# Two experts of a routed layer in passes of 224 and 160 columns, and the conversion of the last weights dealt out anew

## The chip, the cores and the metric

One core of a Trainium2 chip runs the kernel. The metric is the device time of one execution in microseconds; lower is better.

## What is computed

Attention over 4 x 8 heads with a window of 32 around each of 512 local tokens and 32 global tokens (2176 tokens of 512 features in all), then a routed layer of eight experts, then a dense layer with a rational function between its two products. Cut to the part around the change:

```python
e_idx = np.argmax(x @ w_gate, axis=1)
for e in range(E):                      # E = 8
    mask = e_idx == e
    h = np.maximum(x[mask] @ w1[e], 0.0)          # 512 -> 1024
    out[mask] = gate_w[mask, None] * eom[mask, e, None] * (h @ w2[e])   # 1024 -> 512
...
h = x @ w_in                                       # 512 -> 2048
g = P(h) / (Q(h) + 1e-6)
return g @ w_out                                   # 2048 -> 512
```

The reference's inputs (seed 0) route 422, 331, 253, 249, 220, 149, 434 and 118 tokens to the eight experts.

## The kernel before, in words

Every product is made in three parts from a high and a low half of each float32 operand (`fp32r`), so a matrix of weights is first split: ScalarE copies a piece of 128x512 to the high half (line 695), VectorE or GpSimd subtracts to give the low half (line 699, odd pieces on VectorE, even ones on GpSimd).

**Experts.** `expert(e)` (line 1023; the text counts from the first, so e = 4 and 5 are the fifth and sixth) runs one wide pass (`wide`, line 918) over a fixed number of token columns, `wd(e)`: 256, or what `WIDE` (line 43) names. Tokens beyond that are done after it in a branch (`beyond`, line 1031), which is entered only if the count is larger. A pass has eight blocks of hidden features. For block s: 12 matmuls into a PSUM tile `ph` (line 932; there are two such banks), the ReLU on ScalarE (line 937), the low half on VectorE (line 938, which is the last reader of `ph`), and, two blocks later, 12 matmuls of the second product (line 944). At the end ScalarE and VectorE copy the four sums to the tile `yt` (line 950), and ScalarE's queue stores `yt` to memory (line 869, reached from line 954).

**The plan.** While expert e runs, a plan (`PLANW`, line 61) is woven between its matmuls: 32 places, four for each block from the third on (two after each half of the first product, two in the second product). At its places stand: `s` splits the next weights piece of the next expert, whose load SP's queue issues four pieces ahead (line 685); `g` gathers rows of tokens (line 804); `x` and `p` scale, transpose and split tokens for the next expert (lines 816, 829, 809, 810); `c` does one step of the conversion.

**The conversion.** 18 pieces of the last layer's weights come as 64-bit floats and are turned to 32 bits in three VectorE steps each (`conv_step`, line 748; lines 731, 734, 737). After the third step SP's queue stores the piece (line 755) and loads the next but one (line 757). Piece q is written into `self.f32[q % 3 % 2]`: a tile of its own, `f32`, or, where q mod 3 is 1, the first 512 numbers of each partition of `yt` (`spare`, line 1001). The tile framework makes each write wait for the readers of what it overwrites, stores included. Each of the second to seventh expert does three pieces (nine steps), at places 2 to 4, 12 to 14 and 22 to 24; `todo` (line 962) counts on from step 9(e - 1).

```python
self.conv_op(self.r64[q % 2], self.f32[q % 3 % 2], n)
if n == 2:
    CQ(self.nc).dma_start(out=self.wf[q], in_=self.f32[q % 3 % 2].bitcast(F32))
```

Of the kernel before, what the change touches and what calls it, by code (L numbers as in the profile page):

```python
# [24 lines left out]
E = 8  # L25
# [14 lines left out]
NB = 2  # L40
BASE, MOST, LAG = 256, 512, 2
NX = 4
READY, WIDE = (6,), {0: 296, 1: 332, 6: 308}
FIRST = WIDE[0]
SA, S0, S1 = "v", "a", "a"

# [1 line left out]
def plan(n, **at):  # L48

    o = [""] * n  # L50
    for t in "scxpgk":
        for k in at.get(t, ()):
            o[k] += t
    return o


NPRE, NCONV = 2, 9

LOADS = [(f, f + 1) for f in range(0, NPRE, 2)] + [(f,) for f in range(NPRE, 16)]
WLO = lambda nc, f: nc.vector if f < 3 else nc.gpsimd  # L60
PLANW = plan(32, s=range(0, 31, 2), c=(2, 3, 4, 12, 13, 14, 22, 23, 24), g=(1, 3, 18, 24), x=(1, 2, 14, 16), p=(5, 8, 19, 22))
PLANW7 = plan(30, s=(0, 5, 6, 8, 9, 11, 12, 14, 15, 17, 18, 20, 21, 23, 24, 25))
EY = 11, 1, 11, 1
GT = 25, 27
# [39 lines left out]
class Build:  # L104
# [731 lines left out]
    def experts(self, st, first, gate):  # L836
# [8 lines left out]
        wd = lambda e: WIDE.get(e, BASE)  # L845
# [12 lines left out]
        X = lambda e: self.xs if e == 0 else self.xa if e % 2 else self.x2c  # L858
# [8 lines left out]
        def store(e, c, n, y, q):  # L867

            q.dma_start(out=self.ybuf[:, :, bass.ds(off[e] + c, n)], in_=y)
# [48 lines left out]
        def wide(e, n, x, bg, last=True, acc=None, before=None):  # L918

            W = self.slot[e % 2]  # L920
            nh = min(NH, 1 + (NH - 1) * BASE // n)
            rest, bg = bg, iter(()) if before else bg
            acc = [ps_a.tile([128, 512], F32, tag=f"acc{m}", name=f"acc{m}") for m in range(4)] if acc is None else acc
            for s in range(8 + LAG):
                if s == AFTER and before:
                    before()
                    bg = rest
                if s < 8:
                    ph = ps_h.tile([128, 512], F32, tag="ph", name="ph")[:, :n]
                    c = 128 * (s % 4)  # L930
                    for i, (k, a, b) in enumerate(ORDER):
                        nc.tensor.matmul(ph, lhsT=W[:, b, 2 * k + s // 4, c:c + 128], rhs=x[:, a, k, :n],  # L932
                                         start=(i == 0), stop=(i == 11))
                        if i % 6 == 5:
                            next(bg, None)
                    hi, lo = (hT(s % nh, n)[:, a] for a in range(2))
                    nc.scalar.activation(hi, ph, AF.Relu)  # L937
                    nc.vector.scalar_tensor_tensor(out=lo, in0=ph, scalar=0.0, in1=hi.bitcast(F32),
                                                   op0=ALU.max, op1=ALU.subtract)
                if s >= LAG:  # L940
                    f = s - LAG
                    for m in range(4):
                        for i, (a, b) in enumerate(PAIRS):
                            nc.tensor.matmul(acc[m][:, :n], lhsT=W[:, b, 8 + f, 128 * m:128 * m + 128],  # L944
                                             rhs=hT(f % nh, n)[:, a], start=(f == 0 and i == 0), stop=(f == 7 and i == 2))
                        if m % 2:
                            next(bg, None)
            def end():
                for m in range(4):
                    (nc.scalar.copy, nc.vector.tensor_copy)[m % 2](yt[:, m, :n], acc[m][:, :n])  # L950
                k = min(NBLK, 128 - NBLK * e)
                YQ(nc).dma_start(out=self.toks[bass.ds(off[e], 128 * k), :].rearrange("(j p) o -> j (p o)", p=128),
                                 in_=self.idxT[NBLK * e:NBLK * e + k])
                store(e, 0, n, yt[:, :, :n], YQ(nc))

            if last:
                end()
            for _ in bg:
                pass
            return end  # L960

        def todo(e, plan, half=None, blocks=(), gathers=(), mode=SPLIT_MODE):


            sp = self.split_set(e + 1, mode if e < E - 1 else MODE7, half)
            k = NCONV * (e - 1)
            gs, xs, ps, ns = iter(gathers), iter(blocks), iter(blocks), self.counts()
            for do in plan:
                for c in do:
                    if c == "s":  # L970
                        next(sp, None)
                    elif c == "c":
                        self.conv_step(k)
                        k += 1
                    elif c == "k":
                        next(ns, None)
                    elif c == "g":
                        for e2, b, j in filter(None, islice(gs, 1)):
                            self.gather(j, col(e2, b))
                    elif c == "x":  # L980
                        for e2, b, j in filter(None, islice(xs, 1)):
                            self.scale(j, 128, S0 if e == 0 else S1)
                    elif c == "p":
                        for e2, b, j in filter(None, islice(ps, 1)):
                            if e2:
                                self.prep(j, X(e2), ps_t(), 128 * b, scale=False, pt=None if e else next(turns)())
                            elif b == FIRST // 128:
                                self.prep(j, self.xs, ps_t(), 0, scale=False, skip=FIRST % 128, pt=next(turns)())
                            else:
                                self.prep(j, self.xs, ps_t(), 128 - FIRST % 128, FIRST % 128, scale=False, pt=next(turns)())  # L990
                yield

        blocks = lambda e, bs=range(4): [(e, b, b) for b in bs if e < E]

        def fetch(e, i):

            ixo = self.ixo[:, 0:1]
            nc.gpsimd.tensor_copy(ixo, self.idx[:, bass.ds(i + NBLK * e, 1)])
            self.gather(NX - 1, ixo)
# [14 lines left out]
        def weave(*gens):  # L1014
            gens = list(gens)
            while gens:
                for g in list(gens):
                    try:
                        next(g)
                    except StopIteration:  # L1020
                        gens.remove(g)
                yield

        def expert(e, early=lambda: ()):

            plan = PLANW if e < E - 1 else PLANW7
            more_ = blocks(e + 1, (2, 3)) if e + 1 in READY else [None] * 2
            wide(e, wd(e), X(e), weave(todo(e, plan, None, blocks(e + 1, (0, 1)) + more_, more_ + blocks(e + 2, (0, 1))),
                                         iter(early())), before=(lambda: beyond(e - 1)) if e > 1 else second)

        def beyond(e):
            n, end = wd(e), nc.s_assert_within((cnt[e] + 127) // 128, 0, NBLK)

            def blocks_from(j):
                fetch(e, j)
                more(e, j, end)
            with tc.If(cnt[e] > n):
                if e in READY:
                    single(e, n, X(e), n)
                    with tc.If(cnt[e] > n + 128):  # L1040
                        blocks_from((n + 128) // 128)
                else:
                    blocks_from(n // 128)

        def woven():

            g, sp, end = self.gate(B - 1, woven=GW), todo(0, PLANA, 0, mode="act"), object()
            while True:
                more_ = [next(g, end) for _ in range(GS)]
                next(sp, None)  # L1050
                yield
                if end in more_:
                    break
            ready = [(0, 2, 3)] + blocks(1, (0, 1, 2)) + [(0, 3, 3)]
            yield from weave(sp, todo(0, PLANB, 1, ready, ready + blocks(2, (0, 1)), mode=MODEB),
                             self.lists(), todo(0, PLANC))
# [27 lines left out]
        for e in range(1, E - 2):  # L1084
            expert(e)


        def early():
            for n in range(CH[0]):
                for _ in range(EY[n]):  # L1090
                    yield
                self.load_y(n, nc.scalar)
# [21 lines left out]
        def first_w():  # L1114
            for f in range(NPRE):
                w, (hi, lo) = self.raws[9, 0][:, 512 * f:512 * f + 512], (self.slot[1][:, a, f, :] for a in range(2))
                nc.scalar.copy(hi, w)
                nc.vector.tensor_tensor(out=lo, in0=w, in1=hi.bitcast(F32), op=ALU.subtract)

        expert(E - 2, early)  # L1120
        expert(E - 1, lambda: first_steps([0]))
        beyond(E - 1)
# [3 lines left out]
        with tc.If(rare[0] > 0):  # L1126

            k, w = 128 - NBLK * (E - 1), yt.rearrange("p m t -> p (m t)")[:, 0:NCOL - 128]
# [341 lines left out]
```

## Time and profile before

| what | value |
|---|---|
| median of 3 runs | 778.91 us (778.0 to 779.42) |
| the profiled execution | 779.69 us |
| its span, first to last instruction | 778.0 us |
| mean granted clock of TensorE | 0.993 |
| busy: TensorE, VectorE, ScalarE, GpSimd | 757.1, 584.4, 527.3, 352.7 us |
| the passes of the second to eighth expert start at | 181.54, 226.72, 250.47, 274.72, 298.42, 323.52, 351.98 us |
| the last layer's own stage starts at | 394.76 us |

Times below are microseconds from the start of the span. A matmul's end is modelled, and a row of several matmuls runs from the first one's start to the last one's end; two neighbours overlap. The releaser in brackets is what ended the idle time before an instruction.

### The profile page before, as it was taken

How to read it: one execution, taken by the hardware profiler on the slowest of the kernel's cores; microseconds unless marked ns; L12 is line 12 of the kernel's file. 1: busy time of each engine (PE TensorE's matmuls, PEld its weight loads, DVE VectorE, ACT ScalarE, POOL GpSimd, SP SyncE). 2: the span in 40 equal slices, each digit the busy share in tenths (PEclk: the TensorE clock that was granted, in tenths of full speed). 3: DMA queues.
4: the chain of work that ended last, by engine and by line, in shares of the span. 5: the costliest groups of instructions: out<-in, count | busy, mean ns of one | idle time of the engine just before them, and what ended most of it. 6: DMA issues, size and time to landing. Idle time of an engine off the chain costs nothing. (4 is left out here: it accounts for less than half of the span.)

```text
span 778.0 us, 16683 instructions
## 1 busy us (share of the span) xinstructions
PE 757.1 (97%) x5976; PEld 652.5 (84%) x5976; DVE 584.4 (75%) x1419; ACT 527.3 (68%) x1181; POOL 352.7 (45%) x439
## 2 busy tenths in 40 slices
PE   8998999899999999999999999999999999999996
PEld 5776776698999999998978888898888898989984
DVE  5777788683568877772389998888888768997983
ACT  4666775555455656643778887778777767887872
POOL 4445664523255556541756866532342214322422
PEclk9999999999999999999999999999999999999998
DMA  8998885555588999893463340110010000000101
GB/s 290 323 312 273 291 269 144 144 168 184 191 279 285 316 304 334 287 306 114 127 195 109 109 108 1 51 45 14 1 54 14 1 1 27 28 1 1 40 1 40
DMA packets 51978, 112.55 MB, mean 145 GB/s; under 512 B 10194, under 2 KB 24274, under 8 KB 49832
## 3 DMA queue, kind: packets, MB, share of 16 engines
q1 hardware_dynamic: 42232, 96.39, 39.1%
q0 software_dynamic: 3168, 9.27, 3.4%
q10 hardware_dynamic: 6480, 5.65, 2.3%
q8 instruction: 52, 0.85, 0.5%
q14 instruction: 46, 0.38, 0.2%
HBM read 93.58 MB, written 18.77 MB: 144 GB/s over the span
## 5 line engine op out<-in xcount | busy, mean ns | idle before, releaser
L1256 POOL TENSOR_TENSOR q<-q,ab 128x384 f32<-128x384 f32 (+1 forms) x78 | 93.9, 1204 | 212.1 <-ACT q L1255 205.1
L1295 PE MATMUL acc<-slot,gh 128*128 128x512 f32 x528 | 165.7, 394 | 0.0
L699 POOL TENSOR_TENSOR slot<-raw,slot 128x512 fp32r<-128x512 f32 x66 | 90.3, 1377 | 89.0 <-ACT slot L695 86.9
L1150 PE MATMUL ph<-x2c,slot 128*128 128x512 f32 (+1 forms) x552 | 125.1, 374 | 0.9 <-DVEq L1126 0.6
L1150 PEld LDWEIGHTS ph<-x2c,slot 128*128 128x128 f32 x552 | 101.1, 187 | 19.6 <-DVEq L1126 0.9
L1295 PEld LDWEIGHTS acc<-slot,gh 128*128 128x128 f32 x528 | 98.3, 187 | 20.1 <-ACT gh L1267 0.2
L944 PE MATMUL acc<-hT,slot 128*128 128x256 f32 (+3 forms) x768 | 109.2, 292 | 0.0
L1295 PE MATMUL acc<-slot,gl 128*128 128x512 f32 x264 | 104.4, 395 | 0.0
L944 PEld LDWEIGHTS acc<-hT,slot 128*128 128x128 f32 x768 | 101.9, 189 | 0.2
L695 ACT CAST slot<-raw 128x512 fp32r<-128x512 f32 x128 | 75.0, 618 | 7.6 <-DVE yt L950 4.0
L316 POOL TENSOR_SCALAR pr<-ex,r 128x128 f32<-128x128 f32 x128 | 47.0, 379 | 60.8 <-PE sc L263 21.0
L1150 PE MATMUL ph<-xa,slot 128*128 128x384 f32 x384 | 71.8, 336 | 0.0
L1150 PEld LDWEIGHTS ph<-xa,slot 128*128 128x128 f32 x384 | 67.9, 188 | 2.7
L1267 ACT CAST gh<-u 128x384 fp32r<-128x384 f32 (+1 forms) x78 | 43.3, 555 | 39.0 <-PE acc L1295 20.8
L699 DVE TENSOR_TENSOR slot<-raw,slot 128x512 fp32r<-128x512 f32 x62 | 55.0, 890 | 14.9 <-ACT slot L695 14.4
L1270 ACT ACTIVATE r<-q,cab 128x384 f32<-128x384 f32 (+1 forms) x78 | 51.3, 657 | 19.3 <-POOL q L1256 18.7
L937 ACT ACTIVATE hT<-ph 128x256 fp32r<-128x256 f32 (+3 forms) x64 | 25.7, 401 | 50.8 <-PE ph L932 40.1
L1295 PEld LDWEIGHTS acc<-slot,gl 128*128 128x128 f32 x264 | 49.4, 187 | 12.3 <-DVE gl L1268 0.3
L298 ACT ACTIVATE ex<-sm,mx 128x128 f32<-128x128 f32 x128 | 50.3, 395 | 13.9 <-POOL pr L316 7.0
L1255 ACT ACTIVATE q<-ab,cab 128x384 f32<-128x384 f32 (+1 forms) x78 | 58.3, 747 | 0.9
L1255 ACT ACTIVATE u<-ph,cab 128x384 f32<-128x384 f32 (+1 forms) x78 | 55.0, 705 | 4.0 <-POOL gl L1268 2.8
L932 PE MATMUL ph<-xa,slot 128*128 128x256 f32 (+1 forms) x384 | 54.6, 292 | 1.2 <-PEq L1040 0.4
(235 smaller groups left out, 1471.0 us busy)
## 6 DMA issues: line engine op xcount, KB each, us to landing
raw<-in_w_dram SPq DMA_DIRECT2D x78, 512.0 KB
vw<-in_vw_dram SPq DMA_DIRECT2D x16, 1024.0 KB
r<-in_w_dram SPq DMA_DIRECT2D x18, 512.0 KB
kw<-in_kw_dram SPq DMA_DIRECT2D x16, 384.0 KB
raw<-wf SPq DMA_DIRECT2D x9, 512.0 KB
qt<-in_qT_dram SPq DMA_DIRECT2D x32, 128.0 KB
xbuf<-xrow SPq DMA_DIRECT2D x8, 512.0 KB
xg<-ybuf SPq DMA_DIRECT2D x13, 256.0 KB
```

The costliest lines, as they stand in the source:

```text
L298: nc.scalar.activation(ex[:, h], src[:, h], AF.Exp, bias=mx[:, h:h + 1], scale=-1.0, accum_out=ssum[:, h:h + 1])
L316: nc.gpsimd.tensor_scalar(out=pr[:, h], in0=ex[:, h], scalar1=r[:, h:h + 1], scalar2=1.0, op0=ALU.mult, op1=ALU.mult)
L695: nc.scalar.copy(hi, r)
L699: eng.tensor_tensor(out=lo[:, c], in0=r[:, c], in1=hi[:, c].bitcast(F32), op=ALU.subtract)
L932: nc.tensor.matmul(ph, lhsT=W[:, b, 2 * k + s // 4, c:c + 128], rhs=x[:, a, k, :n], start=(i == 0), stop=(i == 11))
L944: nc.tensor.matmul(acc[m][:, :n], lhsT=W[:, b, 8 + f, 128 * m:128 * m + 128], rhs=hT(f % nh, n)[:, a], start=(f == 0 and i == 0), stop=(f ...
L1150: self.nc.tensor.matmul(ph[:, :w], lhsT=l[a], rhs=r[b], start=(k == 0 and i == 0), stop=(k == 3 and i == 2))
L1255: nc.scalar.activation(o_, x_, AF.Identity, scale=k1, bias=k0)
L1256: nc.gpsimd.tensor_tensor(out=q, in0=q, in1=ab, op=ALU.mult)
L1267: nc.scalar.copy(g[0], up)
L1270: nc.scalar.activation(r0, q, AF.Ln, bias=eps1)
L1295: nc.tensor.matmul(accs[i], lhsT=l[a], rhs=Wo[:, b, f, :], start=(f == 0 and j == 0), stop=(f == 15 and j == 2))
```

## The change

The fifth and sixth expert's passes are 224 and 160 columns wide instead of 256. The conversion is dealt out 4, 3, 3, 2, 2, 4 to the second to seventh expert instead of three to each, at the places that `EACH` gives for the number of pieces. `pair` names the token blocks that an expert has; for every width here it gives the same two as before.

```diff
-READY, WIDE = (6,), {0: 296, 1: 332, 6: 308}
+READY, WIDE = (6,), {0: 296, 1: 332, 4: 224, 5: 160, 6: 308}
...
-NPRE, NCONV = 2, 9
+NPRE = 2
+PIECES = 0, 4, 3, 3, 2, 2, 4, 0
...
-PLANW = plan(32, s=range(0, 31, 2), c=(2, 3, 4, 12, 13, 14, 22, 23, 24), g=(1, 3, 18, 24), x=(1, 2, 14, 16), p=(5, 8, 19, 22))
+EACH = {4: (2, 8, 14, 20), 3: (2, 12, 22), 2: (3, 10), 0: ()}
+PLANW = lambda e: plan(32, s=range(0, 31, 2), c=[k + n for k in EACH[PIECES[e]] for n in range(3)], g=(1, 3, 18, 24), x=(1, 2, 14, 16), p=(5, 8, 19, 22))
...
-            k = NCONV * (e - 1)
+            k = 3 * sum(PIECES[:e])
...
+        pair = lambda e: blocks(e, range(min(2, -(-wd(e) // 128)))) + [None] * (wd(e) <= 128)
...
-            plan = PLANW if e < E - 1 else PLANW7
+            plan = PLANW(e) if e < E - 1 else PLANW7
             more_ = blocks(e + 1, (2, 3)) if e + 1 in READY else [None] * 2
-            wide(e, wd(e), X(e), weave(todo(e, plan, None, blocks(e + 1, (0, 1)) + more_, more_ + blocks(e + 2, (0, 1))),
+            wide(e, wd(e), X(e), weave(todo(e, plan, None, pair(e + 1) + more_, more_ + pair(e + 2)),
```

## Rows read from the trace of the kernel before

**Rows 1.** Stretches of four experts: length; PE, PEld, DVE, ACT, POOL; PEclk, DMA, GB/s

```profile
250.35:274.60 24.25, 24.10 (x203) 23.93 (x201) 19.03 (x30) 14.28 (x31) 13.90 (x11) 1.00 0.92 312
274.60:298.30 23.70, 23.55 (x203) 23.38 (x202) 19.12 (x30) 14.27 (x31) 13.81 (x11) 1.00 0.91 308
298.30:323.40 25.10, 24.95 (x211) 24.78 (x209) 20.20 (x32) 16.63 (x35) 16.78 (x12) 1.00 0.96 331
323.40:351.84 28.44, 28.29 (x203) 28.06 (x201) 20.17 (x30) 15.12 (x31) 12.66 (x10) 1.00 0.90 280
```

**Rows 2.** What PE waited for from 195 to 400 us, the longest of five

```profile
PE ph L1150 <- DVEq L1126: 0.6, 1, 0.6
```

**Rows 3.** Timeline: groups of 12 matmuls; last, durations of single ones of L932

```profile
212.12 1.99 PE L932 MATMUL ph<-xa,slot 128*128 128x332 f32 x12
...
285.70 1.59 PE L944 MATMUL acc<-hT,slot 128*128 128x256 f32 x12
287.12 1.54 PE L932 MATMUL ph<-x2c,slot 128*128 128x256 f32 x12
...
308.28 1.60 PE L932 MATMUL ph<-xa,slot 128*128 128x256 f32 x12
...
L932 PE MATMUL ph<-xa,slot x384: 276/283/419, 181.5 to 390.0; 128*128 128x256 f32 x144, 128*128 128x332 f32 x48
```

**Rows 4.** Timeline of weight loads where PE's stream starts anew, and of transposes (L829)

```profile
367.24 0.19 PEld L932 LDWEIGHTS ph<-xa,slot 128*128 128x128 f32 x1 [0.67 <-issue]
...
367.24 0.30 PEld L932 LDWEIGHTS ph<-xa,slot 128*128 128x128 f32 x2 [0.67 <-issue]
...
176.06 0.20 PEld L829 LDWEIGHTS ph<-ident,xg 128*128 128x128 f32 x2 [0.58 <-issue]
...
180.94 0.14 PEld L829 LDWEIGHTS pt<-ident,xg 40*128 40x128 f32 x1 [0.32 <-ACT xg L816]
...
180.94 0.32 PEld L829 LDWEIGHTS pt<-ident,xg 40*128 40x128 f32 x4 [0.32 <-ACT xg L816]
```

**Rows 5.** DMA queue q10 (ScalarE's): 261.9 to 262.0; 284.7 to 284.9; 227.9 to 234.5

```profile
q10 hardware_dynamic: 2, 0.00, 3.4%
...
q10 hardware_dynamic: 1, 0.00, 0.3%
...
q10 hardware_dynamic: 546, 0.69, 31.4%
```

**Rows 6.** Timeline of the fourth expert's first half: start, us, engine, line

```profile
251.23 0.39 ACTq L869 DMA_DIRECT2D ybuf<-yt  x1
...
255.49 0.42 DVE L731 TENSOR_SCALAR f<-r 128x512 int32<-128x512 int32 x1
...
255.95 0.69 DVE L734 SCALAR_TENSOR_TENSOR f<-r,f 128x512 int32<-128x512 int32 x1
...
257.60 0.42 DVE L938 SCALAR_TENSOR_TENSOR hT<-ph,hT 128x256 fp32r<-128x256 f32 x1 [0.95 <-ACT hT L937]
...
260.35 1.60 PE L932 MATMUL ph<-xa,slot 128*128 128x256 f32 x12
...
262.79 0.42 DVE L731 TENSOR_SCALAR yt<-r 128x512 int32<-128x512 int32 x1
```

**Rows 7.** Timeline of the fifth and the third expert: the store, hidden block 4

```profile
275.49 0.39 ACTq L869 DMA_DIRECT2D ybuf<-yt  x1
...
284.34 1.52 PE L932 MATMUL ph<-x2c,slot 128*128 128x256 f32 x12
...
227.56 0.40 ACTq L869 DMA_DIRECT2D ybuf<-yt  x1
...
236.37 1.54 PE L932 MATMUL ph<-x2c,slot 128*128 128x256 f32 x12
```

**Rows 8.** Two stretches of the attention stage, columns as in rows 1

```profile
67.45:70.86 3.41, 1.54 (x58) 1.15 (x54) 2.07 (x13) 0.80 (x5) 1.46 (x4) 1.00 0.73 260
70.86:74.27 3.41, 3.41 (x35) 2.33 (x35) 1.55 (x8) 1.73 (x8) 1.15 (x3) 0.50 0.45 56
```

## Prediction

> **What bounds the kernel now.** I read the table of stretches first, one row for each expert. The engine columns show TensorE busy for all of every stretch but 0.15 us, VectorE for about four fifths, the DMA engines for 0.90 to 0.96 [rows 1]. Next came what TensorE waited for between 195 and 400 us: five rows, none above 0.6 us [rows 2]. So the experts are paced by the matmul stream, and VectorE and the DMA engines have little to spare. Anything that makes the stream shorter is gained one for one; anything that makes TensorE wait for VectorE is paid one for one.
>
> The stream's pace comes from the groups of 12 matmuls. One matmul reads 0.28 us by itself, 12 read 1.54 to 1.60, so consecutive ones start (1.54 - 0.28)/11 = 115 ns apart in the first product of the fifth expert, 119 in its second, 120 in the sixth; 332 columns give (1.99 - 0.32)/11 = 152 [rows 3], where 0.32 is an estimate from 0.28 and the 76 added columns.
>
> **Narrower passes.** A matmul has its own weight load in this kernel, so the pace has a second limit that a narrow pass does not touch. The trace of before has no such matmul under 256 columns. It does show the load's length: where the stream starts anew, one load reads 0.19 us and two read 0.30, so the second began 0.11 us after the first [rows 4]. A transpose's load is lighter, two in 0.20 [rows 4], that is 0.14 and 0.06. And one place shows what happens when the load outlasts the stream: the 40-column transposes stream for about 20 ns (40/256 of 119), yet their four loads take 0.32 us, (0.32 - 0.14)/3 = 0.06 apart [rows 4]. That is the load's own 0.06, not the stream's 0.02 and not the sum of both. By this the pace falls to the load's 108 to 110 ns and stops there; with a few ns of handover I take 112, whether 224 columns follow or 160.
>
> Each of the two experts has 96 first-product and 96 second-product matmuls. Fifth: 96 x (115 - 112) + 96 x (119 - 112) = 1.0 us. Sixth: 192 x (120 - 112) = 1.5 us. Gain 2.5 us. Lower bound nothing (the pace stays at 119); upper bound in proportion to the columns, 104 and 75 ns: 192 x 13 + 192 x 45 = 11.1 us. But in the sixth the DMA engines bind before that: 331 GB/s for 25.1 us are 8.3 MB [rows 1]; less one converted piece (0.52 MB read, 0.26 MB written) 7.5 MB, 22.7 us at the same rate, so that expert can hardly give more than 2.4 us, and the upper end with DMA is 2.5 + 2.4 = 4.9 us. I take 2.5 because the nearest row with a load longer than its stream follows the load.
>
> The Trainium skill, page "TensorE: Matmul & The Clock Gate", section "Back-to-back issue gap", gives N/2.4 + 2.5 ns for warm matmuls. By that the gaps would be 96 and 69 ns and the gain, as an estimate from that page, 4.0 + 9.8 = 13.8 us; the rows at 256 columns stand at 115 to 120 where it says 109, so the trace does not bear it out here.
>
> The smaller ReLU, subtraction and copies on ScalarE and VectorE gain nothing: TensorE does not wait for them [rows 2]. The smaller stores of those two experts are off the path.
>
> **Pieces dealt anew.** One piece is three VectorE instructions, 0.42, 0.69 and about as much again, a 256 KB store and a 512 KB load on SP's queue. The fifth and sixth lose one each, some 1.8 us of VectorE and 0.79 MB, hidden by TensorE before, so worth nothing by themselves. The second and seventh gain one. The second's stretch is not among the rows; the seventh has 28.44 - 20.17 = 8.3 us of VectorE idle and 280 GB/s where the sixth reached 331 [rows 1]: hidden. Its second piece rewrites the same buffer four plan places after the first; if the store of it is late, VectorE waits, at most by what it has idle: 0, up to 0.5 us for TensorE.
>
> What counts is which buffer each piece uses. Piece q goes to the spare part of yt where q mod 3 is 1. Before, that was the middle piece of each expert, places 12 to 14. With 4 pieces ahead of the third expert the order shifts: pieces 4, 7 and 10 become the FIRST of the third, fourth and fifth expert, at places 2, 2 and 3. But yt is what the expert before has just stored from, and the write must wait for that store. VectorE takes its instructions in order; behind the waiting one stand the subtraction of hidden block 2 (line 938), then the input splits and weight splits. TensorE's hidden block 4 needs the PSUM bank that line 938 frees (two banks).
>
> Fourth expert: the store is issued at 251.23, its last packets move at 261.9 to 262.0 [rows 5], and the old middle piece wrote yt at 262.79 [rows 6]. So the store is done between 262.0 and 262.8; I take 262.4. The new first piece would be due at 255.49 [rows 6]: 6.9 us of wait. Then 0.42 + 0.69, line 938 with 0.42 and 0.1 of gaps: the bank is free at 264.0, where TensorE took it at 260.35 [rows 6]: 3.7 us of stall. The next bank comes after some 2.6 us more of VectorE (five operations like these) against 24 x 0.12 = 2.9 us of TensorE: 0.3 us more at crowded moments. Together 4.0.
>
> Fifth: stored from 275.49, last packets at 284.8 [rows 5, 7], done by 285.2 if as late as in the fourth. At place 3 only one operation stands ahead of line 938: 285.2 + 0.42 + 0.42 + 0.1 = 286.1 against 284.34 [rows 7], less 0.3 that the narrower pass has gained by then: 2.1. Then four more operations of 0.69 and one of 0.42, 3.3 us with gaps, against 24 x 0.112 = 2.7: 0.6. Together 2.7.
>
> Third: stored from 227.56, all 546 packets through by 234.5 [rows 5, 7], done at 234.8; line 938 ends at 236.4 against 236.37 [rows 7]. So 0 at first, 0.4 with crowding after it.
>
> Sum of the stalls 7.1 us. Lower bound: if every store took as little from issue as the third's 7.2 us (227.56 to 234.8), the fourth would be done at 258.4 and the fifth at 282.7, both early enough that TensorE sees nothing: 0. Upper bound: TensorE idle for 3.7 us in one go may lower its clock. After a stretch with 1.54 us of matmuls in 3.41 the granted clock stood at 0.50, the 1.2 GHz level, for 3.41 us [rows 8]; that costs 1.7 us, twice 3.4.
>
> In the sixth, piece 13 writes yt at place 10, about when the store lands there too; what VectorE waits there TensorE does not see, since it needs that bank only a whole block later.
>
> **Sum.** 779.69 (the profiled execution, of which 778.0 are the span) - 2.5 + 7.1 = 784.3; the median of the runs is 0.8 below the profiled one, so 783.5.
>
> **Rivals.**
> The store lands sooner, or VectorE catches up before TensorE looks (the other side). Place: the first piece of the fourth expert. For it: one of the three stores took 7.2 us. Against it: the two that matter took 11.2 and 9.7 under the load that stays there. It decides at 258.7: a store done by then (260.35 less 1.6) costs nothing. Then only the narrow passes are left, with 0.2 of stall: 778.9 - 2.3 = 776.6. Chance 0.17.
>
> The passes go by their columns. For it: 332 to 256 columns is nearly proportional [rows 3]. Against it: the load's 0.11 and the 40-column transposes. With the stalls: 778.9 - 4.9 + 7.1 = 781.1 if DMA binds, 774.9 if it does not. Chance 0.10, of which 0.04 ends below the old time. This is where the rule of the Trainium skill's page would lead.
>
> The stall lowers the clock, or late weight loads follow it (the buffers that VectorE frees late are SP's next loads): 783.5 + 1.7 to 3.4, so 785.2 to 786.9. For it: the row at 0.50 [rows 8]. Against it: the stretch before it held attention's short matmuls, not these. Chance 0.20.
>
> Extra blocks because 224 and 160 are too few: the reference's inputs route 220 and 149 tokens there, so left out.
>
> **Numbers.** Forecast 0.48; the rest 0.05 on either side. A change under 0.2% (1.6 us) is about what a measurement of this kernel cannot tell from none. Faster: most of the first rival's 0.17, 0.04 and a little of the rest, 0.22. Same: 0.10, the part of the forecast and of the second rival between 777.4 and 780.5. Slower 0.68. The range 776.5 to 787.5 takes in the first rival's point, the forecast with stalls of 3 to 9 us, and one clock drop with late loads. The forecast's own range is 780.5 to 786.
>
> **What would show it.** Right: in the third, fourth and fifth expert the first write of yt from the conversion stands right after the store's last packet, with VectorE idle 3, 7 and 5.5 us ahead of it; TensorE then waits for line 938 about 4 us in the fourth and 2 to 3 in the fifth; 12 matmuls of 160 columns read about 1.45 us, as do those of 224. Wrong: no wait of TensorE over 1 us between 226 and 300, or 12 matmuls of 160 columns in 1.1 us or less, or the sixth expert still at 25 us.

## The result, and the profile after

| | median | lowest to highest |
|---|---|---|
| before, 6 runs | 778.45 us | 776.36 to 779.88 |
| after, 6 runs | 803.89 us | 788.76 to 813.81 |

The change makes the kernel slower. The six executions fall in two groups, 788.76 and 789.55 us with a mean granted clock of 0.99 and four from 803.01 to 813.81 us with 0.96 to 0.97; the ratio of the first two to before is 1.0141 [1.0105, 1.0178] (in brackets the 95% interval, here and below), that of the medians 1.033. The profiled execution (806.0 us, span 804.3) is one of the four. Its lower clock belongs to the result: the experiments show that the change brings it about. Lines of the kernel are two further down in the profile after: the first product is line 934, the low half 940, the second product 946.

Where the time went is read from the starts of the passes:

| start of | before | after | later by |
|---|---|---|---|
| third expert | 226.72 | 224.02 | -2.70 |
| fourth | 250.47 | 254.24 | 3.77 |
| fifth | 274.72 | 279.32 | 4.60 |
| sixth | 298.42 | 305.63 | 7.21 |
| seventh | 323.52 | 349.01 | 25.49 |
| eighth | 351.98 | 378.31 | 26.33 |
| last layer | 394.76 | 421.11 | 26.35 |

The 2.7 us ahead of the third expert are not a gain of the change: 2.62 of them lie ahead of the second expert (178.92 against 181.54), in stages that it doesn't touch, and the second, which now converts four pieces, took 45.10 us against 45.18. The third expert lost 6.5, the fourth 0.8, the fifth 2.6, the sixth 18.3, the seventh 0.8.

The table of stretches of the kernel after, third to sixth expert, answers to [rows 1] (length, busy time of PE, PEld, DVE, ACT and POOL with counts, PEclk, DMA share, GB/s). The last two rows are the two stretches at a granted clock of 0.50:

```profile
224.02:254.24 30.22, 25.13 (x203) 24.55 (x201) 20.00 (x29) 14.62 (x31) 13.48 (x10) 0.96 0.75 256
254.24:279.32 25.08, 24.80 (x201) 24.43 (x201) 19.82 (x27) 14.38 (x30) 12.97 (x10) 0.98 0.86 278
279.32:305.63 26.31, 23.46 (x203) 22.68 (x201) 18.65 (x29) 13.08 (x28) 12.25 (x10) 1.00 0.82 264
305.63:349.01 43.38, 42.03 (x211) 41.75 (x209) 16.76 (x28) 17.07 (x37) 17.20 (x13) 0.55 0.59 192
...
251.83:255.24 3.41, 3.30 (x15) 3.30 (x16) 2.11 (x5) 0.74 (x2) 0.00 (x0) 0.50 0.60 184
309.86:350.82 40.96, 40.83 (x191) 40.83 (x192) 15.88 (x28) 15.55 (x33) 15.92 (x12) 0.50 0.53 165
```

The third expert before, which [rows 1] leaves out:

```profile
226.60:250.35 23.75, 23.60 (x202) 23.43 (x202) 19.37 (x29) 14.42 (x31) 12.57 (x11) 1.00 0.87 292
```

The rows tell two stories. In the third and fifth expert TensorE is idle for 5.1 and 2.9 us, and the DMA share is 0.75 and 0.82 where it was 0.87 and 0.91: something waits. In the sixth TensorE is idle for 1.4 us only, but its clock is 0.55: everything it does takes longer.

**The waits.** What TensorE waited for between 195 and 400 us, where before nothing was above 0.6 us [rows 2]:

```profile
PE acc L946 <- DVE hT L940: 3.1, 1, 3.1
PE ph L934 <- DVE hT L940: 3.0, 2, 1.9
PE ph L934 <- DVEq L1041: 2.6, 2, 1.4
```

They are found in the timeline, with what stands ahead of them (VectorE's rows, then two of GpSimd and one of ScalarE, then TensorE's; in brackets the idle time before the instruction and what ended it):

```profile
233.36 1.22 DVE L733 TENSOR_SCALAR yt<-r 128x512 int32<-128x512 int32 x1 [4.25 <-DMA ybuf<-yt]
248.91 1.92 DVE L733 TENSOR_SCALAR f<-r 128x512 int32<-128x512 int32 x1 [2.69 <-DMA wf<-f]
261.10 1.06 DVE L733 TENSOR_SCALAR yt<-r 128x512 int32<-128x512 int32 x1 [1.30 <-DMA raw<-in_w_dram]
277.89 2.52 DVE L739 SCALAR_TENSOR_TENSOR f<-r,f 128x512 int32<-128x512 int32 x1
289.92 1.33 DVE L733 TENSOR_SCALAR yt<-r 128x512 int32<-128x512 int32 x1 [3.89 <-DMA raw<-in_w_dram]
...
249.26 1.27 POOL L701 TENSOR_TENSOR slot<-raw,slot 128x512 fp32r<-128x512 f32 x1
289.69 1.27 POOL L701 TENSOR_TENSOR slot<-raw,slot 128x512 fp32r<-128x512 f32 x1 [1.65 <-ACT slot L697]
...
282.25 0.62 ACT L697 CAST slot<-raw 128x512 fp32r<-128x512 f32 x1 [2.71 <-DVE yt L952]
...
235.69 1.65 PE L934 MATMUL ph<-x2c,slot 128*128 128x256 f32 x12 [1.86 <-DVE hT L940]
251.94 2.50 PE L946 MATMUL acc<-hT,slot 128*128 128x256 f32 x10 [3.08 <-DVE hT L940]
283.95 1.60 PE L934 MATMUL ph<-x2c,slot 128*128 128x224 f32 x12 [1.40 <-DVEq L1041]
291.60 1.60 PE L934 MATMUL ph<-x2c,slot 128*128 128x224 f32 x12 [1.17 <-DVE hT L940]
```

The writes at 233.36, 261.10 and 289.92 are the forecast ones: the first piece of the third, fourth and fifth expert goes to yt and waits for the store from it. (For the last two the view names a weights load as the releaser; the semaphore of the store from yt is set at 261.08 and 289.89, the same moments.) The write at 248.91 was not forecast: pieces 5 and 6 both go to `f`, and piece 6 waits until piece 5 has been stored. Behind it TensorE waits longest, 3.08 us. The wait of 1.40 us at 283.95 has no such write ahead of it: the third step of piece 9, at the end of the fourth expert, took 2.52 us, the copies to yt came after it, ScalarE waited 2.71 us for them, and its ReLU was late.

Part of these stalls is slower work and not waiting. The first step of a piece takes 0.42 us [rows 6], but 1.92 us at 248.91 and 1.33 at 289.92: GpSimd was at work when they began, and each ended 0.3 us after GpSimd's subtraction. Between 180 and 350 us of all the profiles here, the 178 first steps that began while GpSimd was idle took 0.41 to 0.43 us. By that, some 1.5 of the 3.08 us (an estimate, 1.92 less 0.42) are the slower step. No experiment moved GpSimd's work.

The waiting piece also holds up SP's queue. SP's rows of the fifth expert in the kernel after:

```profile
286.12 0.33 SPq L687 DMA_DIRECT2D raw<-in_w_dram  x1
292.90 0.33 SPq L757 DMA_DIRECT2D wf<-yt  x1
293.28 1.27 SPq L759 DMA_DIRECT2D r<-in_w_dram  x1
294.65 1.81 SPq L687 DMA_DIRECT2D raw<-in_w_dram  x2
```

and in the kernel before, in the same expert:

```profile
284.19 5.64 SPq L685 DMA_DIRECT2D raw<-in_w_dram  x3
290.05 0.33 SPq L755 DMA_DIRECT2D wf<-yt  x1
```

After, the store of the piece is next in the queue, its data come late, and SP issues nothing for 6.4 us; the weight loads stand behind it. Before, three loads went out in that time. The queue is not all that held them: there are four weight buffers, and the one that the load at 294.65 fills was still to be read by VectorE's subtraction at 293.39 to 294.07, which itself stands behind the write to yt.

**The clock.** The sixth expert's beginning after (first what stands ahead of the late weight load, then ScalarE, VectorE, TensorE), and a later group of 12 matmuls:

```profile
298.77 0.68 DVE L701 TENSOR_TENSOR slot<-raw,slot 128x512 fp32r<-128x512 f32 x1
298.88 0.33 SPq L757 DMA_DIRECT2D wf<-f  x1
299.78 10.32 SPq L687 DMA_DIRECT2D raw<-in_w_dram  x5
...
306.78 0.62 ACT L697 CAST slot<-raw 128x512 fp32r<-128x512 f32 x1 [3.58 <-DMA raw<-in_w_dram]
308.88 0.30 ACT L939 ACTIVATE hT<-ph 128x160 fp32r<-128x160 f32 x1
309.62 0.32 DVE L940 SCALAR_TENSOR_TENSOR hT<-ph,hT 128x160 fp32r<-128x160 f32 x1
...
309.99 2.85 PE L934 MATMUL ph<-xa,slot 128*128 128x160 f32 x12 [1.20 <-DVEq L1041]
332.10 2.76 PE L934 MATMUL ph<-xa,slot 128*128 128x160 f32 x12
```

ScalarE waits 3.58 us for a weights piece, the ReLU behind it in ScalarE's order is late, and TensorE stands for 1.2 us. The load of that piece went out at 299.78 and landed at 306.70: VectorE's subtraction at 298.77 was the last to read its buffer, and the store of the converted piece went out ahead of it at 298.88. Where TensorE starts again, from 309.86, the granted clock is 0.50, the 1.2 GHz level. Consecutive matmuls then start 213 ns apart (median) for the whole pass, and the clock is back to full only at 350.82, 1.8 us after the seventh expert's 308-column pass has begun.

### The profile page after: what moved, and what is told of

Read it like the earlier page. It is cut to its first block, busy times and chain, and to the rows that moved or that the text cites. A ratio compares the mean times of both kernels' runs of the same rounds, so it can differ in the third digit from the quotient of the medians.

```text
span 804.3 us, 16690 instructions
## 1 busy us (share of the span) xinstructions
PE 775.1 (96%) x5976; PEld 670.3 (83%) x5976; DVE 585.0 (73%) x1419; ACT 526.5 (65%) x1181; POOL 349.8 (43%) x439
## 5 line engine op out<-in xcount | busy, mean ns | idle before, releaser
L701 POOL TENSOR_TENSOR slot<-raw,slot 128x512 fp32r<-128x512 f32 x66 | 88.2, 1345 | 120.5 <-ACT slot L697 116.2
L946 PE MATMUL acc<-hT,slot 128*128 128x256 f32 (+5 forms) x768 | 119.3, 310 | 3.2 <-DVE hT L940 3.1
L946 PEld LDWEIGHTS acc<-hT,slot 128*128 128x128 f32 x768 | 111.8, 209 | 3.8 <-DVE hT L940 3.6
L1154 PEld LDWEIGHTS ph<-xa,slot 128*128 128x128 f32 x384 | 67.9, 188 | 2.7
L939 ACT ACTIVATE hT<-ph 128x256 fp32r<-128x256 f32 (+5 forms) x64 | 24.8, 388 | 62.6 <-PE ph L934 45.9
L934 PE MATMUL ph<-xa,slot 128*128 128x256 f32 (+2 forms) x384 | 62.0, 318 | 2.3 <-DVEq L1041 1.2
L1274 ACT ACTIVATE r<-q,cab 128x384 f32<-128x384 f32 (+1 forms) x78 | 51.2, 657 | 19.1 <-POOL q L1260 18.3
L934 PEld LDWEIGHTS ph<-xa,slot 128*128 128x128 f32 x384 | 58.4, 219 | 3.5 <-DVEq L1041 1.4
```

What stands on the lines that cost most here:

```text
L701: eng.tensor_tensor(out=lo[:, c], in0=r[:, c], in1=hi[:, c].bitcast(F32), op=ALU.subtract)
L1154: self.nc.tensor.matmul(ph[:, :w], lhsT=l[a], rhs=r[b], start=(k == 0 and i == 0), stop=(k == 3 and i == 2))
L1274: nc.scalar.activation(r0, q, AF.Ln, bias=eps1)
```

## Experiments

They undo or isolate the two parts, widths and dealing, then each kind of wait, and then put a pause of TensorE where the clock fell. The kernel before that stands beside each run was timed on the same chip.

### The narrow passes with the old dealing

```diff
-READY, WIDE = (6,), {0: 296, 1: 332, 6: 308}
+READY, WIDE = (6,), {0: 296, 1: 332, 4: 224, 5: 160, 6: 308}
```

> The new widths (224, 160) with the conversion dealt out as before. Waiting theory (the added time is VectorE waiting to write yt): no such wait is left, so 2.5 us faster than before, the sixth expert at about 23.6 us. Clock theory (the 160-column pass, paced by its weight loads, lets the granted clock fall to 0.50): the sixth expert takes about 43 us where that happens, as after the change, so 16 us slower in such an execution; the matmuls stand 213 ns apart there.

Measured: 776.82 us (774.91 to 778.49, 10 runs) against 777.74; ratio 0.9991 [0.9975, 1.0006]. A group of 12 matmuls of 160 columns:

```profile
307.47 1.50 PE L932 MATMUL ph<-xa,slot 128*128 128x160 f32 x12
```

Consecutive ones start 112 ns apart at 160 columns and 111 at 224 (medians). The sixth expert took 24.77 us. In all ten executions the mean granted clock is 0.992 or more: without the new dealing it stayed up here (in a run below with the same widths and dealing, the short pause, one execution of ten lost it). The time is not the 2.5 us less that were expected: the interval reaches from 1.9 us less to 0.5 us more.

### 224 columns in the fifth expert alone

```diff
+READY, WIDE = (6,), {0: 296, 1: 332, 4: 224, 6: 308}
```

> The fifth expert alone at 224 columns, everything else as before. Weight-load theory: its matmuls go from 115 and 119 ns to 112 apart, 1.0 us faster in all. Columns theory: 104 ns, 2.5 us faster. Clock theory: no fall at 224 columns, so the same as the weight-load theory.

Measured: 777.62 us (776.76 to 779.59, 10 runs), ratio 1.0005 [0.9986, 1.0023]. The fifth expert's stretch is 22.70 us long against 23.70 [rows 1]: the forecast 1.0. Over the whole kernel that is less than the measurement can tell.

### The new dealing with the old widths

The kernel after, with `WIDE` as before.

> The conversion dealt out anew, all widths as before. Waiting theory: 7 to 11 us slower than before, in the third to fifth expert, with VectorE idle before the first write of yt. Clock theory: the sixth expert stays near 25 us with the granted clock at 1.00. If the dealing costs nothing, same as before.

Measured: 784.82 us (784.19 to 787.56, 4 runs), ratio 1.0093 [1.0069, 1.0117]. The dealing alone makes about 7 us of the loss. In its profile TensorE waits for the reuse of `f`: 0.68 us behind piece 6 and 3.07 us (at 278.67, in the fourth expert) behind piece 9, which reuses `f` after piece 8. There the clock stood at 0.50 for 6.83 us, with 256 columns, and came back. The write to yt in the fourth kept VectorE 3.09 us, and TensorE did not wait for it.

### The new dealing with each expert's second piece in yt

```diff
+CB = 0, 1, 0, 0, 0, 1, 0, 0, 1, 0, 0, 1, 0, 1, 0, 0, 1, 0
...
-        self.conv_op(self.r64[q % 2], self.f32[q % 3 % 2], n)
+        self.conv_op(self.r64[q % 2], self.f32[CB[q]], n)
```

(and the same in the store). The widths are 224 and 160. In the seventh expert it is the third of the four pieces.

> The changed kernel, but each expert's second piece is the one that goes to yt, as before the change (third to sixth expert: own tile, yt, own tile). Waiting theory: the waits of the third to fifth expert are gone, 7 to 11 us less than the changed kernel; without a fall of the clock 2.5 us faster than before. Clock theory: the sixth expert still takes about 43 us in the executions in which the clock falls. DMA theory (the moved traffic is what costs): no gain against the changed kernel.

Measured: 775.52 us median (773.71 to 793.46, 10 runs); ratio 0.999 [0.9961, 1.002] without the longest. The third and fourth expert in the table of stretches:

```profile
223.80:247.50 23.70, 23.55 (x202) 23.38 (x201) 19.25 (x29) 14.37 (x31) 12.23 (x10) 1.00 0.87 298
247.50:271.80 24.30, 24.15 (x203) 23.98 (x202) 19.30 (x30) 14.28 (x31) 14.28 (x10) 1.00 0.91 312
```

Their lengths, TensorE's time and the DMA share are those of before [rows 1]. So the number of pieces for each expert costs nothing that can be told; the buffer of each piece does. The sixth expert took 23.63 us. One execution of the ten took 793.46 us with a mean granted clock of 0.972; no execution with 224 or 256 columns went so low, so a pass of 160 columns seems to lose the clock now and then even here. That execution has no profile. Another took 783.52 us at 0.993, which stays unexplained.

### The new dealing with 224 and 256 columns

```diff
-READY, WIDE = (6,), {0: 296, 1: 332, 4: 224, 5: 160, 6: 308}
+READY, WIDE = (6,), {0: 296, 1: 332, 4: 224, 6: 308}
```

> The new dealing, fifth expert at 224 columns, sixth back at 256. Theory (stalls by the reused buffers cost about 7 us; the fall of the clock to 0.50 that lasts 41 us needs the 160-column pass of the sixth expert): 783 to 785 us, about 1 below the 784.8 of the new dealing with 256 and 256, no stretch at 0.50 between 220 and 350 us longer than 7 us, in any run. Rival (the stalls alone make the clock stay low, the width has no part in it): some runs above 795 us with a mean granted clock of 0.97, as with 160 columns.

Measured: 785.14 us (784.11 to 787.01, 4 runs), ratio 1.0083 [1.0051, 1.0115], so not the 1 us under the new dealing alone that was expected. In the profile the clock fell once among the experts, for 3.41 us, behind a wait of 3.09 us in the third. The stalls are there, the long fall is not: the mean clock is 0.990 to 0.994 in all four. Only the width of the sixth expert differs from the kernel after. But TensorE's wait at the sixth's beginning is shorter here too, 0.41 us; the version with the scratch tile, below, has the longer one.

### A pause of TensorE before 160, 256 and 224 columns

The old dealing; the low half of the sixth expert's first block is written 12 times, so that TensorE waits for VectorE.

```diff
-                    nc.vector.scalar_tensor_tensor(out=lo, in0=ph, scalar=0.0, in1=hi.bitcast(F32),
-                                                   op0=ALU.max, op1=ALU.subtract)
+                    for _ in range(12 if (e, s) == (5, 0) else 1):
+                        nc.vector.scalar_tensor_tensor(out=lo, in0=ph, scalar=0.0, in1=hi.bitcast(F32),
+                                                       op0=ALU.max, op1=ALU.subtract)
```

> The old dealing with 224 and 160 columns, and the low half of the sixth expert's first tile written 12 times in place of once, so that TensorE waits some 2.5 us for VectorE early in that expert's pass. Theory (a pause lets the granted clock fall, and a 160-column pass does not bring it back): 0.50 for the rest of the pass, some 20 to 35 us of matmuls 213 ns apart, and 776.8 + 2.5 + 12 to 20 = 791 to 799 us. Rival (a pause costs its length and one stretch of 3.41 us at most): 779 to 782 us.

> The same pause, with the sixth expert at 256 columns. Theory: the clock falls for one or two stretches of 3.41 us and comes back within the pass, so 777.6 + 2.5 to 3 + 1.7 to 3.4 = 781 to 784 us. Rival (any pause at this place keeps the clock low, whatever the width): above 790 us, as with 160 columns.

> The pause of before (the sixth expert's first low half written 12 times), with the sixth expert at 224 columns, which run at the same pace of 111 to 112 ns as 160 at the full clock. Theory (it is how few columns stand behind one weight load that keeps the clock down, and 224 are enough): the clock comes back within the pass, 780 to 785 us, as with 256 columns (782.4). Rival (any pass that is bound by its weight loads stays at 0.50 after a pause): 795 us or more, as with 160 columns (798.7).

| columns of the sixth expert | median | lowest to highest | runs | ratio to before |
|---|---|---|---|---|
| 160 | 798.67 | 796.0 to 804.19 | 4 | 1.0244 [1.0209, 1.0279] |
| 224 | 784.46 | 784.17 to 787.23 | 4 | 1.0082 [1.0061, 1.0104] |
| 256 | 782.43 | 779.73 to 786.25 | 10 | 1.0052 [1.0033, 1.0071] |

The pause was about twice as long as meant, and of similar length in the three. TensorE's wait with 160 columns, and the stretches from its fall on:

```profile
PE ph L932 <- DVEq L1038: 5.4, 1, 5.4
...
302.99:346.03 43.04, 39.02 (x184) 39.02 (x185) 20.83 (x40) 14.68 (x32) 15.53 (x12) 0.50 0.61 200
350.78:376.51 25.73, 25.73 (x185) 25.73 (x185) 18.51 (x26) 13.13 (x27) 11.19 (x8) 1.00 0.72 232
```

With 256 columns:

```profile
PE ph L932 <- DVEq L1038: 4.6, 1, 4.6
...
306.94:310.35 3.41, 3.41 (x18) 3.41 (x17) 2.70 (x6) 2.20 (x5) 0.00 (x0) 0.50 0.65 213
310.35:330.07 19.72, 19.72 (x168) 19.72 (x167) 14.86 (x23) 12.14 (x25) 11.28 (x8) 1.00 0.73 244
```

With 224 columns:

```profile
PE ph L932 <- DVEq L1038: 5.2, 2, 4.4
...
304.94:311.77 6.83, 5.53 (x26) 5.53 (x27) 4.28 (x9) 2.35 (x5) 2.00 (x2) 0.50 0.85 306
311.77:329.98 18.21, 17.94 (x160) 17.75 (x159) 14.36 (x20) 11.93 (x25) 9.97 (x8) 1.00 0.73 241
```

The PEclk column decides it. After nearly the same pause the clock is back within the pass with 256 and 224 columns, and not with 160: there it rose only at 350.78, in the pass that follows, as in the kernel after. The pause before 160 columns was the longest of the three, but in the kernel after 1.2 us came ahead of the same long fall. The mean clock of all their executions agrees: 0.963 to 0.971 with 160 columns, 0.991 or more with the others. The rival that any pass bound by its weight loads stays down falls with the 224 columns, which go at 111 to 112 ns too.

### A short pause before 160 columns

The same edit with 3 in place of 12.

> The pause at the start of the sixth expert's 160-column pass again, on the old dealing, but short: the first low half is written 3 times in place of 12, so that TensorE waits some 1 to 2.5 us, near the 1.2 us that it waited there in the kernel of the change. Theory (such a short pause is enough to let the clock fall in some executions, and 160 columns then keep it down): part of the runs at 792 to 797 us with a mean granted clock of 0.97, the others at 777.5 to 779.5 with 0.99 or more. Rival (only a pause of several us does it, so that something else must have added to it in the kernel of the change): all runs below 781.

Measured: 775.93 us median (774.39 to 797.35, 10 runs), ratio 0.9971 [0.9951, 0.9991]. VectorE had more to spare there than I allowed for: in the profile no wait of TensorE between 195 and 400 us is above 0.7 us, so the pause that was meant wasn't made. One execution, 797.35 us at a mean clock of 0.973, lost the clock all the same; it has no profile. The ratio is that of the other nine. How short a pause is enough stays open.

### A scratch tile of its own for pieces 6 and 9

```diff
+    def buf(self, q):
+        return self.hr[1].bitcast(I32) if q in (6, 9) else self.f32[q % 3 % 2]
```

used in `conv_step` in place of `self.f32[q % 3 % 2]`, with the new dealing and 224 and 256 columns. It takes the wait of `f` for `f` away and leaves the writes to yt as the first piece.

> As the new dealing with 224 and 256 columns (785.14), but pieces 6 and 9, the last of the third and fourth expert, are converted into a scratch tile of their own instead of the buffer that the piece before them still stores from; the writes to yt as the first piece stay. Theory (two waits share the cost: yt behind the ybuf store, and the write of a last piece behind the store of the piece before it, the second costing 3 to 4 us in the third or fourth expert): 781 to 782.5 us, no waits of TensorE over 1 us late in the third and fourth expert, the waits on yt stay. Rival (only the yt writes cost): 785, unchanged. Other rival (only the reused f32 costs): 777 to 778.5.

Measured: 784.52 us (779.91 to 789.42, 7 runs), ratio 1.0089 [1.0051, 1.0127]: by the median nothing was won, which is the first rival's number, but the trace shows another reason. Third and fourth expert, VectorE's and TensorE's row, and SP's queue at the fourth's beginning:

```profile
223.60:248.46 24.86, 24.71 (x209) 24.54 (x208) 20.28 (x30) 14.95 (x32) 14.41 (x10) 1.00 0.82 272
248.46:277.83 29.37, 25.82 (x202) 25.43 (x201) 18.43 (x30) 14.13 (x31) 13.39 (x12) 0.94 0.79 283
...
244.78 0.41 DVE L733 TENSOR_SCALAR hr<-r 128x512 int32<-128x512 int32 x1
...
260.34 0.43 DVE L733 TENSOR_SCALAR yt<-r 128x512 int32<-128x512 int32 x1 [6.72 <-DMA ybuf<-yt]
...
261.88 2.93 PE L937 MATMUL ph<-xa,slot 128*128 128x256 f32 x12 [3.40 <-DVE hT L943]
...
248.56 5.47 SPq L687 DMA_DIRECT2D raw<-in_w_dram  x3
262.45 0.33 SPq L760 DMA_DIRECT2D wf<-yt  x1
```

Piece 6 no longer waits and the third expert's pass is nearly undisturbed (24.86 us from 1.0 us ahead of the first matmul). But VectorE's wait for yt in the fourth grew to 6.72 us and TensorE's to 3.40. From the issue of that store to the write is 11.1 us here (issued at 249.21) and was 6.1 in the kernel after (255.04 to 261.10). The longer the third expert took, the shorter was VectorE's wait for yt in the fourth: 23.86 us and 6.72 here, 24.68 and 3.09 with the new dealing at 256 and 256 columns, 27.09 and 2.56 at 224 and 256, 30.22 and 1.30 after. So a stall upstream makes the later one shorter, and taking the first away gave it to the second. Again SP's queue issues nothing behind the waiting piece, from 254.0 to 262.45.

This profile also answers what the run at 224 and 256 columns left open. At the sixth expert's beginning ScalarE waits 3.83 us for a weights piece and TensorE 1.29 us, as in the kernel after (3.58 and 1.20). Ahead of 256 columns the clock stayed at 1.00:

```profile
302.45:329.12 26.67, 25.23 (x210) 24.85 (x209) 17.97 (x28) 17.55 (x37) 15.82 (x13) 1.00 0.87 293
...
303.85 0.62 ACT L697 CAST slot<-raw 128x512 fp32r<-128x512 f32 x1 [3.83 <-DMA raw<-in_w_dram]
...
307.15 1.70 PE L937 MATMUL ph<-xa,slot 128*128 128x256 f32 x12 [1.29 <-DVEq L1044]
```

### Two kinds of wait away, and no 160

The version with the second piece in yt, `5: 224` in place of `5: 160`.

> The new dealing with the second piece of each expert as the one that goes to yt, and 224 columns for fifth and sixth. Theory (224 and 160 columns have the same pace of 112 ns, set by the weight load; the stalls come from the choice of buffers alone): 774.5 to 776.5 us, as with 160 columns there (775.5), and no run above 780. Rival (160 columns are faster in themselves, or 224 in the sixth doesn't end the falls of the clock): 776.5 or more, or single runs above 785.

Measured: 776.32 us (774.59 to 780.35, 12 runs), ratio 0.9981 [0.9963, 0.9999]. It is the one version with the new dealing that is ahead of the kernel before, by 0.2% and only just clear of the noise. One execution is 0.35 us above the expected bound of 780. None of the 12 lost the clock as the 793.46 above did (0.993 or more). Against 160 columns in the same version (775.52) there is no difference to be told, as the equal pace says.

## Why the prediction was wrong

The direction was right (slower, 0.68), the size was not: 783.5 was forecast with a range to 787.5; the median is 803.89, and even the two executions at a mean clock of 0.99 are above the range, at 788.8 and 789.6.

**Narrower passes: the pace right, the gain in part.** Pace 112 ns forecast, 111 to 112 measured for both widths. The fifth expert gained 1.0 (forecast 1.0). The sixth gained 25.10 - 24.77 = 0.3 with the narrow passes alone, where TensorE's waits took the rest of the forecast 1.5, and 25.10 - 23.63 = 1.5 with the second piece in yt, where it had none. Over the whole kernel the forecast was 2.5 us; the widths alone came out 0.7 us faster than before (0.9991), and 2.3 us faster with the short pause that wasn't made (0.9971). The rival that the passes go by their columns is out.

**Pieces dealt anew, waits on yt: right in kind, in size only in the fourth expert.** The version with the scratch tile shows them without the other wait: in the fourth expert VectorE idle 6.72 us where 6.9 was worked out, TensorE 3.40 where 3.7 was; the store took 11.1 us to the write, where 11.2 was read off. In the fifth TensorE waited 1.16 us for 2.7. In the kernel after itself the fourth's was only 1.3 us of VectorE and none of TensorE. There the store took 6.1 us; the DMA engines had been busy for only 0.60 just before it (251.83:255.24), so fewer transfers may have stood ahead of it, which is a reading and was not tried. In the third, where 0.4 was forecast, TensorE waited 1.86 us: the store took 8.5 us to the write (from 224.86) for the 7.2 worked out, and the write 1.22 us for 0.42.

**The step that failed first: "What counts is which buffer each piece uses".** I followed only the pieces in yt. The same shift puts pieces 5 and 6, and 8 and 9, into `f` one after the other within one expert, so the later must wait for the earlier one's store. I saw this for the seventh expert, where it is hidden, and not for the third, where TensorE waited 3.1 us after the change, or the fourth, where it waited 3.1 with the old widths. I also left out what stands behind the waiting piece: on VectorE the subtractions that free the weight buffers, on SP's queue its own store and then the next weight loads. The sum of the stalls was close with the old widths: the new dealing alone came out 7 us slower, where 7.1 was forecast, but in other places and with the clock's share in it. In the kernel after the third, fourth, fifth and seventh expert together lost 10.7.

**The step that cost most: "The stall lowers the clock, or late weight loads follow it".** As a rival it had both halves of what happened, and a chance of 0.20. Its price was wrong: one or two stretches of 3.41 us, 1.7 to 3.4 us in all, from rows of the attention stage [rows 8]. That was about the price with 224 and 256 columns behind the pause (3.41 or 6.83 us at 0.50). In the 160-column pass the clock stayed down for 40.96 us, and the sixth expert took 43.38 us against 24.77 with the clock up: 18.6 us. I had costed the width of the sixth expert only as a gain and the clock only at the place of the forecast stall, in the fourth; the two meet in the sixth.

**Not settled.** The trace shows what the late weights piece of the sixth expert stood behind, VectorE's subtraction and SP's store; neither was taken away by itself. Why the clock stays down with 160 columns and not with 224 is not shown, only that it does. And the two executions at 0.99 have no profile, so how their 10 to 11 us divide is not shown.

## What to carry to other kernels

When work is dealt to stages anew, list for every reused buffer who wrote it last, when that store lands, and what stands behind the waiting instruction on its engine and behind its store on the DMA queue; an index like q mod 3 changes its meaning with every count ahead of it. When two such waits lie in one stream, removing one may only lengthen the other, so remove them together. And a pass that is bound by its weight loads gains nothing from fewer columns, but may lose much: the passes of 224 and 160 columns ran at the same pace, and only the narrower one stayed at the lower clock after a pause. Price a pause ahead of such a pass with the clock down to its end.

## What the runs showed of the hardware

At the lower clock the pace is 213 ns whether a matmul has 160, 224 or 256 columns (medians in the pauses' profiles and in the kernel after), against 112, 111 and 120 at the full clock. With 308 columns, at the start of the seventh expert after, it is 258 ns, in proportion to 256 columns at 213. So at the lower clock the weight load sets the pace of the narrower matmuls; its limit goes from 112 to 213 ns with half the clock, and there it is about as long as the stream of 256 columns. The Trainium skill, page "TensorE: Matmul & The Clock Gate", section "Back-to-back issue gap", gives N/1.2 for an isolated matmul at the lower level, by which 160 columns would take an estimated 133 ns; the runs show 213 in this stream, where every matmul has a load of its own.

At the full clock the 112 ns are near what the Trainium skill, page "TensorE: Matmul & The Clock Gate", section "LDWEIGHTS (loading the stationary operand)", gives: P/1.2, an estimated 107 ns for 128 columns; the trace agrees to within 5 ns.

Whether the clock came back within the pass differed with its width: after a pause of 4.4 to 5.4 us it was back after 3.41 us with 256 columns and 6.83 with 224, and not within 43 us with 160, in one profile each.

A first step of the conversion on VectorE that began inside a subtraction of GpSimd lasted until 0.3 us after that one's end: 1.06 to 1.33 us for five of them in the kernel after, 0.42 by itself.
